# One place each for keys, values and weights of attention in a fused decode block

## The chip, the cores and the metric

One core of a Trainium2 chip runs the kernel. The metric is device time in microseconds of one execution, as the median of several runs; lower is better. The engines named below are TensorE (PE, with its weight loads PEld), VectorE (DVE), ScalarE (ACT), GpSimd (POOL) and the engine that issues most DMAs, SyncE (SP).

## The reference

Four tokens (batch 4, one query each) pass a layer norm. The result feeds two branches, and the output is their sum with the input:

```
xn  = layernorm(x)                                  # [4, 512]
q   = xn @ wq                                       # 32 heads of 128
k,v = the last 4096 positions of the caches         # 8 key/value heads, each serves 4 query heads
o   = softmax(q k^T / sqrt(128)) v
out = x + o @ wo + (silu(xn @ w_gate) * (xn @ w_up)) @ w_down    # F = 1792
```

All inputs are bf16. The kernel reads 8 groups (key/value heads) of 4 MB of K and 4 MB of V, 4 MB each of wq and wo, and 1792 KB each of w_gate, w_up and w_down: 81 MB.

## The kernel before, in words

A group is one key/value head for all four batches. Its K lies in SBUF as 128 partitions by 128 tiles of 128 elements; its V likewise. For each group there is one pass:

- **Keys.** In 16 chunks of 8 tiles TensorE transposes K into PSUM (`transposes`, L436), DVE or ACT copies the chunk to SBUF (L346, L286; every third one is ACT's), and TensorE forms the scores (`scores`, L445) into four PSUM banks, two chunks behind the transposes. DVE takes the maximum of each bank (L350).
- **Values of the group before.** TensorE sums the probabilities (`den`, L453) and multiplies them with V (`pv`, L459, 64 matmuls), with the transpose of the new maxima (L489) after the first 24. Then it adds the negated maxima to the scores as a product with a mask (L493), ACT exponentiates the banks into P (L289), and `sums` (L466, L468) with DVE normalizes the output of the group before.

So K of pass r and V of group r-1 are used in pass r. The first pass runs its values step on a P of ones, with whatever lies in the V place; that result is overwritten. After the loop one more values step does group 7.

K, V and P have two places each, taken in turn by even and odd groups. The first place of V is `vbuf0`; the second is the place of wq, whose name the trace keeps (`wq_sb`). WO is loaded into the first place of K.

SP issues all loads in one order: WQ, X, WG, WU, K 0, K 1, V 0, then K r and V r-1 for r = 2 to 7, then V 7 in two halves, WD, and WO in five parts. A load of K waits until the transposes of the group two before are done (L238, on `s_tr`), a load of V until the product of the group two before is done (L246 and L251, on `s_pv`). SP issues in order: while it waits, nothing behind it is issued. Issued transfers run one behind another.

Ahead of the loop: the layer norm on DVE, the query product (L410) and its transposes, then the gate product and the up product (L423), the gating on ACT and DVE (L281 to L335, on all 512 columns) and the transposes to `guT` (L429). TensorE starts the first keys when `guT` is ready.

Behind the loop: the output is transposed and spread to `OP` (L508, L512, L388), the products with WD (L518) and with the first 16 rows of WO (L526) collect in one bank, which is folded (L531), and the last 16 rows of WO are added (L538). SP stores the result (L272).

Of the kernel before, what the change touches and what calls it, by code (L numbers as in the profile page):

```python
# [5 lines left out]
ALU = mybir.AluOpType  # L6
# [4 lines left out]
def bass_parallel_sum__sliding_block_cached__swiglu_ffn__decode_kernel(  # L11
# [28 lines left out]
    HALF = NT // 2  # L40
    SCALE = float(Dh) ** -0.5
# [7 lines left out]
    WQ = sb("wq_sb", [128, NC, HQ * Dh], BF16)  # L49
    KB = [sb("kbuf%d" % s, [128, NT, Dh], BF16) for s in range(2)]  # L50
    VB0 = sb("vbuf0", [128, NT, Dh], BF16)
# [18 lines left out]
    P = [sb("p%d" % s, [128, NT, CQ], BF16) for s in range(2)]  # L70
    ex = P[0][:, 0:NT // 2, :].rearrange("p t c -> p (t c)").bitcast(FP32)
    gs = P[0][:, NT // 2:, :].rearrange("p t c -> p (t c)").bitcast(FP32)
    gu = KT[1][:, 0:4, :].rearrange("p k d -> p (k d)")
# [76 lines left out]
    s_gu = sem("s_gu")  # L150
# [4 lines left out]
    s_tr = [[sem("s_tr%d_%d" % (g, n)) for n in range(NCH)] for g in range(2)]
    s_ev = [[sem("s_ev%d_%d" % (g, n)) for n in range(NCH)] for g in range(2)]
    s_sc = [[sem("s_sc%d_%d" % (g, q)) for q in range(NB)] for g in range(2)]
    s_sh = [[sem("s_sh%d_%d" % (g, q)) for q in range(NB)] for g in range(2)]
    s_xp = [[sem("s_xp%d_%d" % (g, q)) for q in range(NB)] for g in range(2)]
    s_cm = [sem("s_cm%d" % g) for g in range(2)]  # L160
    s_mt = [sem("s_mt%d" % g) for g in range(2)]
    s_dd = [sem("s_dd%d" % g) for g in range(2)]
    s_pv = [sem("s_pv%d" % g) for g in range(2)]
    s_oc = [sem("s_oc%d" % g) for g in range(2)]
    s_sl = [sem("s_sl%d" % g) for g in range(2)]
    s_nm = [sem("s_nm%d" % g) for g in range(2)]
# [23 lines left out]

    def run_gpsimd(eng):
        for t in (ident, identf, I4, I48, Lsel, sel2, mxd, Dsh, I4w):
            eng.memset(t[:], 0.0)
# [8 lines left out]
                          fill=1.0, base=0, channel_multiplier=1)  # L202
        eng.memset(OP[:], 0.0)
        eng.memset(P[1][:], 1.0)
        eng.drain()
        eng.affine_select(I48[0:16, :], I48[0:16, :], pattern=[[-1, CQ]], compare_op=ALU.not_equal,
                          fill=1.0, base=0, channel_multiplier=1)
        eng.drain()
        eng.affine_select(I48[32:48, :], I48[32:48, :], pattern=[[-1, CQ]], compare_op=ALU.not_equal,
# [24 lines left out]
    def run_sync(eng):  # L234
        def load_k(r):
            if r >= 2:
                eng.wait_ge(s_tr[r % 2][NCH - 1], r // 2)
            eng.dma_start(KB[r % 2][:].rearrange("p t d -> p (t d)"), kv_ap(A_k_cache, r)).then_inc(d_k[r % 2], 16)  # L238

        def load_v(r, half=None):  # L240
            dst = VB[r % 2].rearrange("p t d -> p (t d)")
            src = kv_ap(A_v_cache, r)
            if r == 1:
                eng.wait_ge(s_q, 1)
            if r >= 1 and half != 1:
                eng.wait_ge(s_pv[(r - 1) % 2], (r - 1) // 2 + 1)  # L246
            if half is None:
                eng.dma_start(dst, src).then_inc(d_v[r % 2], 16)
            else:
                n = HALF * Dh  # L250
                eng.dma_start(dst[:, half * n:(half + 1) * n], src[:, :, half * n:(half + 1) * n]).then_inc(  # L251
                    d_vb if half else d_v[r % 2], 16)
# [3 lines left out]
        eng.dma_start(WG[:], wg_ap).then_inc(d_wg, 16)
        eng.dma_start(WU[:], wu_ap).then_inc(d_wu, 16)
        load_k(0)
        load_k(1)
        load_v(0)  # L260
        for r in range(2, HKV):
            load_k(r)
            load_v(r - 1)
        load_v(HKV - 1, 0)
        load_v(HKV - 1, 1)
        eng.dma_start(WD[:], wd_ap).then_inc(d_wd, 16)
        for q, (a, b) in enumerate(ROWS):
            if q == 0:
                eng.wait_ge(s_tr[0][NCH - 1], HKV // 2)
            eng.dma_start(WO[:, a:b, :], wo_ap[:, a:b, :]).then_inc(d_wo[q], 16)  # L270
        eng.wait_ge(s_y, 1)
        eng.dma_start(out_ap, y_ap).then_inc(d_out, 16)  # L272
        eng.wait_ge(d_out, 16)

    def run_scalar(eng):
        eng.wait_ge(s_var, 1)
        eng.activation(st_std[:], st_var[:], ACT.Sqrt).then_inc(s_std, 1)
        eng.wait_ge(s_q, 1)
        eng.copy(qs[:, 1, :], ps_S[1][:]).then_inc(s_qs, 1)
        eng.wait_ge(s_g, 1)  # L280
        eng.activation(ex, gate_ps[:], ACT.Exp, scale=-1.0).then_inc(s_ex, 1)  # L281
        with eng.Fori(0, HKV // 2) as i:
            for g in range(2):
                for n in range(2, NCH, 3):
                    eng.wait_ge(s_tr[g][n], i + 1)
                    eng.copy(KT[n % 3][:], kt_ps[n % 3]).then_inc(s_ev[g][n], 1)  # L286
                for q in range(NB):
                    eng.wait_ge(s_sh[g][q], i + 1)
                    eng.activation(P[g][:, q * TB:(q + 1) * TB, :], S_ps[q], ACT.Exp,  # L289
                                   scale=SCALE).then_inc(s_xp[g][q], 1)  # L290
        eng.wait_ge(s_pt, 1)
        eng.copy(part[64:128, :], part_ps[64:128, :]).then_inc(s_ptc, 1)

    def run_vector(eng):
# [44 lines left out]
        eng.tensor_copy(guT[:, 12:NF, :], gT[:, 3, 16 - NF:, :])
        eng.drain().then_inc(s_guT, 1)  # L340
        for s in s_xp[1] + [s_nm[1]]:
            eng.sem_inc(s, 1)

        def evac(i, g, n):
            eng.wait_ge(s_tr[g][n], i + 1)
            eng.tensor_copy(KT[n % 3][:], kt_ps[n % 3]).then_inc(s_ev[g][n], 1)  # L346

        def bank_max(i, g, q):
            eng.wait_ge(s_sc[g][q], i + 1)
            eng.tensor_reduce(mxb[:, q, :], S_ps[q].rearrange("p t c -> p c t"), AX.X, ALU.max)  # L350

        def sums(sems, v):
            s_v, s_o, s_l, s_n, slot = sems
            eng.wait_ge(s_v, v)
            eng.tensor_copy(o4[:], o4_ps)  # L355
            eng.tensor_tensor(dd[:], fold16[:], den_ps.to_broadcast([128, CQ]), ALU.mult)
            eng.drain().then_inc(s_o, 1)
# [3 lines left out]
            eng.tensor_tensor(slot, ot_ps, rden[:], ALU.mult).then_inc(s_n, 1)

        with nc.Fori(0, HKV // 2, engines=bass.OrderedEngineSet([eng.engine]), hint_back_edge=True) as i:
            for g in range(2):
                for n in range(NCH):
                    if n % 3 != 2:
                        evac(i, g, n)
                    if n in (4, 9, 13):
                        bank_max(i, g, n // 4 - 1)
                bank_max(i, g, NB - 1)  # L370
                eng.drain()
                eng.tensor_reduce(mx1[:], mxb[:].rearrange("p q c -> p c q"), AX.X, ALU.max)
                eng.drain()
                eng.tensor_tensor(mxd[:, 0:64].rearrange("p (e c) -> p e c", c=32)[:, :, 0:CQ], bc(mx1[:], 2), bc(mask[:], 2), ALU.add)
                eng.drain().then_inc(s_cm[g], 1)
# [18 lines left out]
    def run_tensor(eng):  # L394
# [180 lines left out]
```

## Time and profile before

| | us |
|---|---|
| median of 3 runs | 198.8 |
| the runs | 197.3 to 198.88 |
| the profiled execution | 198.41 |
| its span, first to last instruction | 195.5 |
| TensorE matmuls busy | 153.4 |
| DVE busy | 109.7 |
| ACT busy | 61.5 |

The profile is of one execution. Its rows give start, length, engine, line, operation, output and input, and in square brackets how long the engine had been idle and what ended the wait. A matmul's end is modelled. `PEclk` is the granted share of the TensorE clock. The name `kbuf` stands for both places of K, and for WO; `wq_sb` for WQ and for V of odd groups.

### The profile page before, as it was taken

Reading aid. Unit: us, or ns where it says so; the run is one execution under the profiler, and the core shown is the slowest. Engines: PE = TensorE matmul, PEld = TensorE weight load, DVE = VectorE, ACT = ScalarE, POOL = GpSimd, SP = SyncE. Lnnn points to the kernel's source line nnn. Section 1 sums busy time; section 2 is a strip of 40 time slices with the busy share of each in tenths; the row PEclk is TensorE's granted clock in tenths of the full one; section 3 lists DMA queues with packets and bytes.
Section 4 is the critical chain, followed back from the end, with each engine's and each line's share of the span. In section 5 each row is a group of like instructions: output and inputs, shape, how many; then the busy total and the mean of one; then the engine's idle time right before and its main releaser. Section 6 shows DMA issues by size and latency. Waiting matters only on the chain.

```text
span 195.5 us, 6723 instructions
## 1 busy us (share of the span) xinstructions
PE 153.4 (78%) x3063; PEld 125.7 (64%) x3063; DVE 109.7 (56%) x223; ACT 61.5 (31%) x78; POOL 10.1 (5%) x31
## 2 busy tenths in 40 slices
PE   0003894899988798999998999999599959996435
PEld 0002310898788668978976987996599659965213
DVE  0025218478577637866875785886278636851210
ACT  2000310244344235426525443551345133512010
POOL 8740000000000000000000000000000000000000
PEclk9999999589999969999999999999889997999855
DMA  6999999999999999999999999999999999999991
GB/s 221 436 422 427 447 456 429 439 429 432 422 426 426 419 426 429 436 436 429 436 436 429 429 429 429 436 429 429 436 436 429 429 429 429 402 429 422 419 398 72
DMA packets 3780, 81.14 MB, mean 415 GB/s; under 512 B 440, under 2 KB 572, under 8 KB 828
## 3 DMA queue, kind: packets, MB, share of 16 engines
q1 hardware_dynamic: 3772, 81.01, 97.1%
q8 instruction: 7, 0.11, 0.2%
q14 instruction: 1, 0.01, 0.0%
HBM read 81.01 MB, written 0.00 MB: 414 GB/s over the span
## 4 chain that ended last, share of the span: by engine, by line
PE 48%; DMA 34%; DVE 9%; issue 3%; ACT 3%; SPq 1%; DVEq 1%
PE ps_kt L436 22%; DMA kbuf<-in_A_wo_dram 16%; DMA kbuf<-in_A_k_cache_dram 12%; PE ps_s L445 10%; DMA x_sb<-in_A_x_dram 6%; PE ps_o L459 4%; ACT kT L286 3%; PE ps_s L493 2%; PE ps_s L423 2%; PE ps_s L410 2%; DVE p L330 2%; DVE mxb L350 1%; PE ps_s L538 1%; PE ps_s L526 1%; PE ps_o L468 1%
## 5 line engine op out<-in xcount | busy, mean ns | idle before, releaser
L436 PE MATMUL ps_kt<-ident,kbuf 128*128 128x128 bf16 x1024 | 80.4, 228 | 5.0 <-DMA kbuf<-in_A_k_cache_dram 4.1
L346 DVE COPY kT<-ps_kt 128x1024 bf16<-128x1024 bf16 x88 | 59.0, 687 | 20.9 <-PE ps_kt L436 18.6
L436 PEld LDWEIGHTS ps_kt<-ident,kbuf 128*128 128x128 bf16 x1024 | 63.0, 102 | 5.3 <-DMA kbuf<-in_A_k_cache_dram 4.3
L286 ACT COPY kT<-ps_kt 128x1024 bf16<-128x1024 bf16 x40 | 40.5, 1012 | 57.2 <-PE ps_kt L436 57.2
L445 PE MATMUL ps_s<-qT,kT 128*128 x1024 | 45.2, 170 | 5.0 <-ACT kT L286 2.2
L445 PEld LDWEIGHTS ps_s<-qT,kT 128*128 128x128 bf16 x1024 | 38.4, 97 | 8.8 <-issue 3.8
L289 ACT ACTIVATE p<-ps_s 128x512 bf16<-128x512 f32 x32 | 16.5, 603 | 34.7 <-PE ps_s L493 34.7
L350 DVE TENSOR_REDUCE mxb<-ps_s 128x16 f32<-128x512 f32 x32 | 21.9, 686 | 5.4 <-PE ps_s L445 4.6
L400 PE MATMUL ps_s<-i,xn 4*128 4x4 f32 x4 | 0.6, 254 | 17.5 <-DVE xn L311 17.5
L400 PEld LDWEIGHTS ps_s<-i,xn 4*128 4x128 f32 x4 | 0.6, 207 | 17.5 <-issue 17.5
L459 PE MATMUL ps_o<-wq_sb,p 128*32 128x256 bf16 x320 | 10.4, 274 | 0.0
L459 PE MATMUL ps_o<-vbuf,p 128*32 128x256 bf16 x256 | 9.5, 296 | 0.0
L493 PE MATMUL ps_s<-dsh,lsel 128*128 128x512 bf16 x32 | 8.6, 392 | 0.0
L459 PEld LDWEIGHTS ps_o<-wq_sb,p 128*32 128x32 bf16 x320 | 7.7, 96 | 0.7
L459 PEld LDWEIGHTS ps_o<-vbuf,p 128*32 128x32 bf16 x256 | 6.5, 103 | 2.1 <-issue 1.1
L355 DVE COPY o<-ps_o 128x256 f32<-128x256 f32 x9 | 3.8, 425 | 6.7 <-PE ps_o L459 6.7
L297 DVE TENSOR_REDUCE st_sum<-x_sb 4x1 f32<-4x512 bf16 x1 | 0.7, 674 | 12.2 <-DMA x_sb<-in_A_x_dram 12.2
L359 DVE RECIPROCAL rden<-ps_o 128x16 f32<-128x16 f32 x9 | 2.3, 257 | 8.9 <-PE ps_o L468 8.9
L453 PE MATMUL ps_o<-ones,p 128*128 128x1 bf16 x144 | 5.0, 163 | 1.2 <-ACT p L289 1.2
L453 PEld LDWEIGHTS ps_o<-ones,p 128*128 128x128 bf16 x144 | 4.4, 96 | 1.8 <-issue 1.3
L468 PE MATMUL ps_o<-fold,o 128*128 128x16 f32 x36 | 5.4, 263 | 0.0
L493 PEld LDWEIGHTS ps_s<-dsh,lsel 128*128 128x128 bf16 x32 | 2.6, 101 | 4.0 <-DVE dsh L381 1.5
(96 smaller groups left out, 81.4 us busy)
## 6 DMA issues: line engine op xcount, KB each, us to landing
kbuf<-in_A_k_cache_dram SPq DMA_DIRECT2D x8, 4096.0 KB, 22.1
vbuf<-in_A_v_cache_dram SPq DMA_DIRECT2D x4, 4096.0 KB, 29.5
wq_sb<-in_A_v_cache_dram SPq DMA_DIRECT2D x3, 4096.0 KB, 22.7
wq_sb<-in_A_wq_dram SPq DMA_DIRECT2D x1, 4096.0 KB, 12.2
wq_sb<-in_A_v_cache_dram SPq DMA_DIRECT2D x2, 2048.0 KB, 20.4
kbuf<-in_A_wo_dram SPq DMA_DIRECT2D x1, 2048.0 KB, 30.5
wg_sb<-in_B_w_gate_dram SPq DMA_DIRECT2D x1, 1792.0 KB, 16.3
wu_sb<-in_B_w_up_dram SPq DMA_DIRECT2D x1, 1792.0 KB, 20.3
```

What stands on the lines that cost most here:

```text
L286: eng.copy(KT[n % 3][:], kt_ps[n % 3]).then_inc(s_ev[g][n], 1)
L289: eng.activation(P[g][:, q * TB:(q + 1) * TB, :], S_ps[q], ACT.Exp, scale=SCALE).then_inc(s_xp[g][q], 1)
L330: eng.reciprocal(ex, ex)
L346: eng.tensor_copy(KT[n % 3][:], kt_ps[n % 3]).then_inc(s_ev[g][n], 1)
L350: eng.tensor_reduce(mxb[:, q, :], S_ps[q].rearrange("p t c -> p c t"), AX.X, ALU.max)
L410: last = mm(ps_S[j][32 * k:32 * k + 32, :], XnT[:, c, :], WQ[:, c, 512 * (4 * j + k):512 * (4 * j + k) + 512], start=(c == 0), stop=(c == ...
L436: last = eng.transpose(kt_ps[n % 3][:, k, :], KB[g][:, 8 * n + k, :], ident[:])
L445: last = mm(S_ps[q][:, 8 * (n % 4) + k, :], KT[n % 3][:, k, :], QT[:, bass.ds(2 * i + g, 1), :, :].rearrange("p o b h -> p (o b h)"), star ...
L453: mm(den_ps, P[e][:, 8 * u:8 * u + 8, :].rearrange("p t c -> p (t c)"), ones[:, 0:1], start=(u == 0), stop=(u == NT // 8 - 1))
L459: last = mm(o4_ps[32 * k:32 * k + 32, :], P[e][:, 2 * u:2 * u + 2, :].rearrange("p t c -> p (t c)"), VB[e][:, 2 * u:2 * u + 2, :].rearrang ...
L468: last = mm(ot_ps, o4[:, 128 * e:128 * e + 128], fold[:, 16 * e:16 * e + 16], start=(e == 0), stop=(e == 1), skip_group_check=True)
L493: mm(S_ps[q], Lsel[:], bc(Dsh[:], TB), start=False, stop=True, skip_group_check=True).then_inc(s_sh[g][q], 1)
```

## The change

- **One place** each for K, V and P; the loop has one group per pass and eight passes. WQ uses the place of V. WO has its own place, and its load waits for nothing.
- **Loads.** X is issued by ACT. WQ and each K come in two halves; the first half of K r waits for the eighth chunk of pass r-1 to be transposed, the second half for the last. V r waits until pass r has multiplied V r-1 (`s_pv` at r+1). The order is WQ, WG, K 0, WU, then K r and V r-1 for r = 1 to 7, then V 7 whole, WD in four transfers (96, 20 and 10 rows, and 2 rows cut in eight pieces each), WO in five.
- **Tail.** The up product, its transposes and the gating run after pass 7 (block `t_up`); the gate product stays in front, but its activation is taken later, after the transpose, on 64 columns. The values step is one block (`t_values`) for all nine uses; the ninth also runs the maxima's transpose and the mask product on stale data, released by two extra increments of DVE. TensorE's loop is written with blocks and branches. The end is a block (`t_tail`) that runs once, with a branch back to itself that is never taken and carries a branch hint.
- **Set-up.** Memsets of OP, P and others move from POOL to DVE.

```diff
-    KB = [sb("kbuf%d" % s, [128, NT, Dh], BF16) for s in range(2)]
-    VB0 = sb("vbuf0", [128, NT, Dh], BF16)
+    KB = sb("kbuf", [128, NT, Dh], BF16)
+    VB = sb("vbuf", [128, NT, Dh], BF16)
+    WO = sb("wo_sb", [128, 32, D], BF16)
...
-    WO = KB[0][:].rearrange("p t d -> p (t d)").rearrange("p (j n) -> p j n", n=D)
+    WQ = VB[:].rearrange("p t d -> p (t d)").rearrange("p (c n) -> p c n", c=NC)
...
-    P = [sb("p%d" % s, [128, NT, CQ], BF16) for s in range(2)]
+    P = sb("p", [128, NT, CQ], BF16)
...
+        def load_ka(r):
+            if r:
+                eng.wait_ge(s_tr[NCH // 2 - 1], r)
+            eng.dma_start(kf[:, 0:n], kv_ap(A_k_cache, r)[:, :, 0:n]).then_inc(d_ka, 16)
+
+        def load_kb(r):
+            if r:
+                eng.wait_ge(s_tr[NCH - 1], r)
+            eng.dma_start(kf[:, n:], kv_ap(A_k_cache, r)[:, :, n:]).then_inc(d_kb, 16)
+
+        def load_v(r):
+            eng.wait_ge(s_pv, r + 1)
+            eng.dma_start(vf, kv_ap(A_v_cache, r)).then_inc(d_v, 16)
+
+        eng.dma_start(WQ[:, 0:2, :], wq_ap[:, 0:2, :]).then_inc(d_qa, 16)
+        eng.dma_start(WQ[:, 2:4, :], wq_ap[:, 2:4, :]).then_inc(d_v, 16)
         eng.dma_start(WG[:], wg_ap).then_inc(d_wg, 16)
+        load_ka(0)
+        load_kb(0)
         eng.dma_start(WU[:], wu_ap).then_inc(d_wu, 16)
...
+        for r in range(1, HKV):
+            load_ka(r)
+            load_kb(r)
             load_v(r - 1)
...
+        load_v(HKV - 1)
+        for u, v in WDROWS:
+            eng.dma_start(WD[u:v], wd_ap[u:v]).then_inc(d_wd, 16)
+        eng.dma_start(WD[126:128].rearrange("p t n -> p (t n)").rearrange("p (s e) -> p s e", s=8),
+                      wd_ap[126:128].rearrange("p t n -> p (t n)").rearrange("p (s e) -> p s e", s=8)).then_inc(d_wd, 16)
...
     def run_scalar(eng):
+        eng.dma_start(X[:], x_ap).then_inc(d_x, 16)
...
-        eng.activation(ex, gate_ps[:], ACT.Exp, scale=-1.0).then_inc(s_ex, 1)
+        eng.copy(gs[:], gate_ps[:]).then_inc(s_gs, 1)
...
+        eng.wait_ge(s_gt, 1)
+        eng.activation(ex[:], every8(gT_ps), ACT.Exp, scale=-1.0).then_inc(s_ex, 1)
+        eng.wait_ge(s_u, 1)
+        eng.copy(us[:], up_ps[:]).then_inc(s_us, 1)
...
+        eng.sem_inc(s_cm, 1)
+        eng.sem_inc(s_dd, 1)
+        sums(LAST + 1, OT[:, LAST, :])
...
+        with nc.body("t_values", valid_engines=me):
+            i = nc.snap(it, min_val=0, max_val=LAST)
+            eng.wait_ge(d_v, 16 * i + 16)
+            for q in range(NB):
+                eng.wait_ge(s_xp[q], i + 1)
+            eng.wait_ge(s_nm, i + 1)
+            for u in range(NT // 8):
+                mm(den_ps, P[:, 8 * u:8 * u + 8, :].rearrange("p t c -> p (t c)"), ones[:, 0:1],
+                   start=(u == 0), stop=(u == NT // 8 - 1))
+            pv(0, 24)
+            eng.wait_ge(s_cm, i + 1)
+            eng.transpose(mx_ps, mxd[:], identf[:]).then_inc(s_mt, 1)
+            pv(24, 64).then_inc(s_pv, 1)
...
+            nc.regs_alu(it, it, 1, op=ALU.add)
+            eng.br_lt(it, HKV, on_true="t_keys", on_false="t_more")
+        with nc.body("t_more", valid_engines=me):
+            eng.br_lt(it, LAST + 1, on_true="t_up", on_false="t_tail")
...
+            nc.regs_alu(once, once, 1, op=ALU.add)
+            eng.br_lt(once, 1, on_true="t_tail", on_false="t_end").branch_hint(loc)
```

More of the change, by code (lines that the diff above doesn't have):

```diff
@@ L149, in bass_parallel_sum__sliding_block_cached__swiglu_ffn__decode_kernel @@
     s_g = sem("s_g")
[L150 removed]
+    s_gs = sem("s_gs")
     s_gt = sem("s_gt")
     s_u = sem("s_u")
+    s_us = sem("s_us")
+    s_ut = sem("s_ut")
     s_ex = sem("s_ex")
     s_guT = sem("s_guT")
[L155 to L166, printed above, removed]
+    s_tr = [sem("s_tr%d" % n) for n in range(NCH)]
+    s_ev = [sem("s_ev%d" % n) for n in range(NCH)]
+    s_sc = [sem("s_sc%d" % q) for q in range(NB)]
+    s_sh = [sem("s_sh%d" % q) for q in range(NB)]
+    s_xp = [sem("s_xp%d" % q) for q in range(NB)]
+    s_cm = sem("s_cm")
+    s_mt = sem("s_mt")
+    s_dd = sem("s_dd")
+    s_pv = sem("s_pv")
+    s_oc = sem("s_oc")
+    s_sl = sem("s_sl")
+    s_nm = sem("s_nm")
     s_rt = sem("s_rt")
@@ L339, in run_vector, with evac @@
[L339 to L349, printed above, removed]
+        for t in s_xp + [s_nm]:
+            eng.sem_inc(t, 1)
+        def evac(i, n):
+            eng.wait_ge(s_tr[n], i + 1)
+            eng.tensor_copy(KT[n % 3][:], kt_ps[n % 3]).then_inc(s_ev[n], 1)
@@ L359, in sums @@
             eng.reciprocal(rden[:], dn_ps)
             eng.drain()
[L361 to L375, printed above, removed]
-                eng.wait_ge(s_mt[g], i + 1)
-                eng.tensor_reduce(nrm[:], mx_ps[0:48, :], AX.X, ALU.max, negate=True)
-                eng.drain()
-                eng.tensor_scalar(Dsh[0:48, :], I48[:], nrm[:, 0:1], None, ALU.mult)
-                eng.drain()
-                eng.scalar_tensor_tensor(Dsh[32:48, :], I48[32:48, :], nrm[32:48, 0:1], Dsh[32:48, :],
-                                         ALU.mult, ALU.subtract).then_inc(s_dd[g], 1)
-                sums((s_pv[g], s_oc[g], s_sl[g], s_nm[g], OT[:, bass.ds(2 * i + g, 1), :].rearrange("p o c -> p (o c)")), i + 1)
@@ L427, in run_tensor @@
-        eng.wait_ge(s_gu, 1)
-        for t in range(4):
-            last = eng.transpose(gT_ps[:, t, :], gu[:, 128 * t:128 * t + 128], ident[:])
-        last.then_inc(s_gt, 1)
-        def transposes(i, g, n):
+                    m = mm(o[32 * k:32 * k + 32, :].rearrange("p (t m) -> p t m", m=128), XnT[:, c, :],
+                           w[:].rearrange("p c (m t) -> p c t m", t=NF)[:, c, T0[k]:T0[k] + 4, :],
+                           start=(c == 0), stop=(c == NC - 1), skip_group_check=True)
@@ L433, in transposes @@
+            return m
+        eng.wait_ge(d_wg, 16)
+        x_times(WG, gate_ps).then_inc(s_g, 1)
+        def transposes(i, n):
             if n == 0:
-                eng.wait_ge(d_k[g], 16 * i + 16)
+                eng.wait_ge(d_ka, 16 * i + 16)
+            if n == NCH // 2:
+                eng.wait_ge(d_kb, 16 * i + 16)
             for k in range(8):
-                last = eng.transpose(kt_ps[n % 3][:, k, :], KB[g][:, 8 * n + k, :], ident[:])
-            last.then_inc(s_tr[g][n], 1)
@@ L462, in pv @@
             return last
-        def sums(s_o, s_l, v):
-            eng.wait_ge(s_o, v)
+        me = bass.OrderedEngineSet([eng.engine])
+        it = nc.alloc_registers("t_i", engines=me)
+        once = nc.alloc_registers("t_once", engines=me)
+        nc.regs_mov(it, 0)
+        nc.regs_mov(once, 0)
+        eng.wait_ge(s_qc, 1)
+        eng.wait_ge(s_gs, 1)
+        nc.br("t_keys", engines=me)
+        with nc.body("t_up", valid_engines=me):
+            for t in range(4):
+                last = eng.transpose(gT_ps[:, 128 * t:128 * t + 128], gs[:, 128 * t:128 * t + 128], identf[:])
+            last.then_inc(s_gt, 1)
+            eng.wait_ge(d_wu, 16)
+            x_times(WU, up_ps).then_inc(s_u, 1)
+            eng.wait_ge(s_us, 1)
+            for t in range(4):
+                last = eng.transpose(uT_ps[:, 128 * t:128 * t + 128], us[:, 128 * t:128 * t + 128], identf[:])
+            last.then_inc(s_ut, 1)
+            nc.br("t_values", engines=me)
@@ new lines, in run_tensor @@
+        with nc.body("t_keys", valid_engines=me):
+            i = nc.snap(it, min_val=0, max_val=HKV - 1)
+            transposes(i, 0)
+            transposes(i, 1)
+            for n in range(NCH):
+                if n + 2 < NCH:
+                    transposes(i, n + 2)
+                scores(i, n)
+            nc.br("t_values", engines=me)
+        with nc.body("t_values", valid_engines=me):
+            i = nc.snap(it, min_val=0, max_val=LAST)
+            eng.wait_ge(d_v, 16 * i + 16)
+            for q in range(NB):
+                eng.wait_ge(s_xp[q], i + 1)
+            eng.wait_ge(s_nm, i + 1)
[6 more added lines that the diff above has]
+            pv(24, 64).then_inc(s_pv, 1)
+            eng.wait_ge(s_dd, i + 1)
+            for q in range(NB):
+                mm(S_ps[q], Lsel[:], bc(Dsh[:], TB), start=False, stop=True,
+                   skip_group_check=True).then_inc(s_sh[q], 1)
+            eng.wait_ge(s_oc, i + 1)
@@ L496, in run_tensor @@
-        last = HKV // 2
-        for q in range(NB):
-            eng.wait_ge(s_xp[1][q], last + 1)
-        eng.wait_ge(d_v[1], 16 * (last + 1))
-        eng.wait_ge(s_nm[1], last + 1)
-        den(1)
-        pv(1, 0, 32)
-        eng.wait_ge(d_vb, 16)
-        pv(1, 32, 64).then_inc(s_pv[0], 1)
-        mm(part_ps[0:32, :], I4w[:], X[:], start=True, stop=False, skip_group_check=True)
-        sums(s_oc[0], s_sl[0], last + 1)
-        eng.wait_ge(s_nm[0], last + 1)
-        eng.transpose(rt_ps, OT[:, 1:, :].rearrange("p r c -> p (r c)"), ident[:]).then_inc(s_rt, 1)
```

279 lines of the change are left out of this document (129 added, 150 removed).

## The prediction

> **What bounds the kernel now.** I read the page first: busy shares, DMA slices, queues.
>
> ```profile
> span 195.5 us, 6723 instructions
> ...
> DMA  6999999999999999999999999999999999999991
> ...
> q1 hardware_dynamic: 3772, 81.01, 97.1%
> ...
> PE 48%; DMA 34%; DVE 9%; issue 3%; ACT 3%; SPq 1%; DVEq 1%
> ```
>
> The kernel's one data queue keeps the 16 DMA engines busy for 97.1% of the span, short only in the first and the last slice. 81 MB must be moved before and after, so a gain can come only from the missing 2.9% (5.7 us), and any hole in the queue is paid in full. The table of stages puts a rate to it, one group of heads to a row, after a row from the start:
>
> ```profile
> 24.44:39.10 14.66, 11.32 (x87) 5.07 (x80) 7.20 (x9) 1.61 (x2) 0.00 (x0) 0.83 1.03 441
> 97.75:117.30 19.55, 18.28 (x421) 16.34 (x419) 14.54 (x28) 8.41 (x11) 0.00 (x0) 1.00 1.00 431
> 139.80:159.25 19.45, 16.96 (x347) 15.29 (x347) 12.07 (x24) 7.12 (x9) 0.00 (x0) 0.91 1.00 431
> 159.25:178.70 19.45, 17.84 (x387) 16.08 (x391) 12.02 (x24) 7.12 (x9) 0.00 (x0) 0.91 1.00 426
> ```
>
> The last two columns are DMA share and GB/s: no idle. TensorE is second, and the timeline shows its room:
>
> ```profile
> 89.26 1.50 PE L436 MATMUL ps_kt<-ident,kbuf 128*128 128x128 bf16 x24
> 104.79 0.60 PE L468 MATMUL ps_o<-fold,o 128*128 128x16 f32 x4
> 105.24 1.50 PE L436 MATMUL ps_kt<-ident,kbuf 128*128 128x128 bf16 x24
> 139.83 2.71 PE L436 MATMUL ps_kt<-ident,kbuf 128*128 128x128 bf16 x24 [2.04 <-DMA kbuf<-in_A_k_cache_dram]
> ```
>
> A pass that waits for nothing goes from 89.26 to 105.24: 16.0 us. Before 139.83 TensorE waits for K 6, and before 159.27 (quoted below) for K 7: landings 19.44 us apart, so 9.72 us for each 4 MB. The chain of waits names TensorE for 48%, because TensorE works off a backlog from its late start until about 139. That is not the bound: the queue was full all the while. I turned next to what the queue's own engine waits for:
>
> ```profile
> SPq L238 <- PE ps_kt L436: 102.0, 6, 43.1
> SPq L251 <- PE ps_o L459: 18.8, 1, 18.8
> ```
>
> These cost nothing now, as the next rows show: K loads need a median 22.1 us from issue to landing, against 12.2 us for the first load, issued to an empty queue. The difference is queueing behind other transfers. That cover is what the change spends.
>
> ```profile
> kbuf<-in_A_k_cache_dram SPq DMA_DIRECT2D x8, 4096.0 KB, 22.1
> wq_sb<-in_A_wq_dram SPq DMA_DIRECT2D x1, 4096.0 KB, 12.2
> wg_sb<-in_B_w_gate_dram SPq DMA_DIRECT2D x1, 1792.0 KB, 16.3
> wu_sb<-in_B_w_up_dram SPq DMA_DIRECT2D x1, 1792.0 KB, 20.3
> ```
>
> **One place for V: the hole near the end.** In the new order V 7 follows V 6 directly, and both go to the same place. V 7 may be issued only when pass 7 has multiplied V 6 (s_pv at 8). WD and WO stand behind that wait on SP, so nothing fills the queue. Before, V 7 had the other place. The price is built from these rows, one pass's values step and the transfer it releases:
>
> ```profile
> 152.63 0.54 PE L453 MATMUL ps_o<-ones,p 128*128 128x1 bf16 x16
> 154.33 1.27 PE L459 MATMUL ps_o<-wq_sb,p 128*32 128x256 bf16 x40
> 155.65 1.18 SPq L251 DMA_DIRECT2D wq_sb<-in_A_v_cache_dram  x2
> 159.27 1.76 PE L436 MATMUL ps_kt<-ident,kbuf 128*128 128x128 bf16 x24 [2.08 <-DMA kbuf<-in_A_k_cache_dram]
> 68.78 2.32 PE L459 MATMUL ps_o<-vbuf,p 128*32 128x256 bf16 x40
> ```
>
> - Denominator and PV: 152.63 to 155.60, 2.97 us at the full clock. The x40 block also appears at 2.32 instead of 1.27 us; the whole step at that pace is about 5.0 us. TensorE will have waited a while for V 6, and after the 2.08 us wait 24 transposes took 1.76 us, not 1.50. I take 3.8, nearer to the fast row.
> - Issue follows the end of PV by 0.05 us (155.60 to 155.65).
> - A transfer into an empty queue lands 12.2 us after issue against 9.72 in stream: 2.5 us of latency, hidden until now.
>
> V 6 lands at 159.27 + 9.72 = 169.0 in both orders, since the bytes ahead of it are the same. The hole is 3.8 + 0.05 + 2.5 = **6.3 us** (5.5 to 7.5).
>
> The other loads into single places are covered. V of a middle group becomes free 3 to 5 us after its landing, plus 2.5 of latency: 5.5 to 7.5, under the 9.72 that the next K needs on the queue. K's first half is free halfway through a keys step and wanted a V transfer later. So passes 2 to 6 stay at the 19.45 us pace. Zero, with 2 us of cover or more.
>
> **The start.** X moves to ACT's queue, the query product starts on half of WQ, gating and the up product leave the front, and POOL's memsets move to DVE. Queries and memsets are covered: keys wait for WG's product anyway, and WQ lands 12.2 us after its issue, ahead of WG; uncovered, the memsets would cost their own length. The queue order becomes WQ, WG, K 0, WU, K 1. Pass 0 starts earlier, but it must now release K 1's place in time:
>
> ```profile
> 1.67 0.35 SPq L256 DMA_DIRECT2D wg_sb<-in_B_w_gate_dram  x1
> 2.06 0.59 SPq L257 DMA_DIRECT2D wu_sb<-in_B_w_up_dram  x1
> 23.86 3.82 PE L423 MATMUL ps_s<-wg_sb,xnT 128*32 128x512 bf16 x16
> 22.07 0.58 ACT L279 CAST kT<-ps_s 128x512 bf16<-128x512 f32 x1 [5.47 <-PE ps_s L410]
> 35.06 2.74 PE L436 MATMUL ps_kt<-ident,kbuf 128*128 128x128 bf16 x24 [0.86 <-DVEq L340]
> 41.69 0.61 PE L436 MATMUL ps_kt<-ident,kbuf 128*128 128x128 bf16 x8
> 47.08 0.61 PE L436 MATMUL ps_kt<-ident,kbuf 128*128 128x128 bf16 x8
> 50.58 1.27 PE L459 MATMUL ps_o<-wq_sb,p 128*32 128x256 bf16 x40
> ```
>
> WG lands at 1.67 + 16.3 = 17.97. Its product takes 3.82, and keys now also wait for ACT's copy of it (s_gs), 0.58 by the nearest row: 22.4. K 0's first half lands 4.86 after WG, at 22.8, so keys start near 22.9 instead of 35.06. Offsets of pass 0 before: eighth chunk transposed after 7.24 us (42.30), last chunk after 12.63 (47.69), PV done after 16.79 (51.85).
> - K 1a: issue at 30.1, landing 2.5 + 4.86 later at 37.5. An unbroken queue would land WU at 32.1 (22.36 before, plus 9.72) and K 1a at 36.9. Hole 0.6.
> - K 1b: issue at 35.5, landing 42.9 against 42.4. Hole 0.5.
> - V 0: issue at 39.7, landing 51.95 against 52.6. No hole.
>
> Together **1.1 us**. Pass 0 began slowly: seven chunks from 35.06 to 41.69, 0.95 us each, then eight to 47.08, 0.67 each. If the gate product leaves the clock high, 2 us go and the holes vanish; if V 1 is late too, they reach 2.
>
> **The tail.** The up product, transposes and gating now run between pass 7 and V 7's landing: a 3.8 us product and small steps within a transfer of 12.2 us. [...] The ninth values step adds a mask product ahead of its sums:
>
> ```profile
> 155.53 1.04 PE L493 MATMUL ps_s<-dsh,lsel 128*128 128x512 bf16 x4
> 156.42 0.33 PE L466 MATMUL ps_o<-dd,onesf 128*128 128x16 f32 x2
> 178.12 1.93 PE L459 MATMUL ps_o<-wq_sb,p 128*32 128x256 bf16 x64
> 180.69 0.39 PE L466 MATMUL ps_o<-dd,onesf 128*128 128x16 f32 x2 [0.32 <-DVEq L357]
> 183.17 1.04 PE L518 MATMUL ps_s<-wd_sb,guT 128*32 128x512 bf16 x14
> 188.10 1.90 PE L526 MATMUL ps_s<-kbuf,oP 128*32 128x512 bf16 x16 [3.88 <-DMA kbuf<-in_A_wo_dram]
> 193.09 0.11 PEld L538 LDWEIGHTS ps_s<-kbuf,oP 128*32 128x32 bf16 x4 [0.20 <-DMA kbuf<-in_A_wo_dram]
> ```
>
> Sums start 0.82 after PV with the mask product (155.60 to 156.42), 0.64 without (180.05 to 180.69): 0.2. From V 7's landing TensorE needs 3 to 5 for PV, 0.25 for the stale transpose, then 4.16 (180.05 to 184.21) + 0.2: ready for WO after 7.6 to 9.6. WO's first part came 9.4 after V 7 (188.10 against 178.7). Zero; 0.5 at the most. The end after the last WO part, 193.09 to 195.5, is unchanged.
>
> **W_down in four parts** (96, 20, 10 and 2 rows, the last cut in eight). The engines do not finish together now:
>
> ```profile
> 191.00:192.00 1.00, 1.00 (x40) 0.96 (x32) 0.00 (x0) 0.00 (x0) 0.00 (x0) 0.50 0.49 187
> 192.00:193.10 1.10, 1.10 (x44) 0.63 (x35) 0.00 (x0) 0.00 (x0) 0.00 (x0) 0.50 0.16 56
> ```
>
> Idle share 0.51 x 1.0 + 0.84 x 1.1 = 1.4 us per engine: the most that a better split could gain. Against it, one WD row is 14 KB and takes an engine 0.53 us at 431/16 GB/s; two extra rows on some engine cost 1.07. The hole before V 7 lets every engine run dry and start level, so an unevenness gathered earlier is gone when WD comes. I take 0 (-1.4 to +1.07).
>
> K and WQ in halves: the stage with V 7 in halves took the same 19.45 us as the one before. Zero.
>
> **Sum.** 6.3 + 1.1 = 7.4 us on the profiled execution. That took 198.41 us with a span of 195.5, so 2.9 lie around the span; it stands 0.4 below the median 198.8. 198.41 + 7.4 = **205.8**, span 202.9.
>
> **Rivals.**
> - *The overlap pays for the hole (not slower).* TensorE starts 12 us earlier and is never behind, and the chain gives it 48%. If TensorE were the pace, those 12 us would cover the 7.4: bounded by the queue's missing 5.7 us, of which the first latency 2.5 and the end 2.4 stay, it gives 197.6 to 198.4. It decides if the DMA share in the middle stages falls below 0.97 now; they show 1.00. 0.05.
> - *Passes become TensorE-paced (slower still).* Eight loop edges instead of four, jumps between blocks, and two waits per pass that may lower the clock. A pass from a cold start (139.83, 159.27) takes about 17.3 of 19.45; a further 2.1 us per pass uses up the room. With 3 us, 7 passes lose 0.9 each: 212. Against it: at the loop edge between 104.79 + 0.60 and 105.24 TensorE loses nothing. 0.07. [...]
> - *The queue runs faster* with level engines: 81 MB at the 441 GB/s of the quoted early stretch take 4.3 us less than at 431, so 201.5. Later stages don't hold it. 0.03.
> - *Two engines carry two WD rows more.* From a level start they end the last transfer 1.07 us later: 206.9. It lies inside the forecast; for it: 20 and 10 rows do not divide by 16; against: how rows fall on engines is in no row here. 0.25 of the forecast's 0.80. [...]
>
> **Numbers.** Forecast 0.80 with its own range: 198.41 + 5.5 - 1.4 = 202.5 at the low end, 198.41 + 7.5 + 2.0 + 0.5 + 1.07 = 209.5 at the high. Outcomes not named, 0.05. The range 202.5 to 209.5 leaves out about 2 in 10. The runs before spread by 0.8%, so 1% is about what can be told from no change: faster 0.03, same 0.05, slower 0.92.
>
> **What would show it.** One slice of DMA share near 0 around 170 to 176, with SP's longest late wait at V's load ending on PV; V 7 landing 15 to 17.5 us after V 6; smaller dips at 30 to 38; middle stages at 1.00; up and gating finished before V 7 lands. No hole there would overturn the prediction; a middle share under 0.95 would mean passes are TensorE-paced.

## The result

| | before | after |
|---|---|---|
| median, us | 198.05 | 214.53 |
| runs, us | 196.97 to 198.88 | 214.16 to 216.69 |
| profiled execution, us | 198.41 | 216.69 |
| its span, us | 195.5 | 215.4 |

The ratio is 1.085 (95% interval 1.077 to 1.094): slower, as forecast, but by 16.5 us instead of 7.4, and outside the range of 202.5 to 209.5. The profiled execution is the slowest of the after runs, 2.2 us above their median.

The page of the changed kernel:

```profile
span 215.4 us, 6817 instructions
...
DMA  6999998999999999999999999999999806999892
GB/s 241 435 436 437 414 408 341 365 432 411 420 441 444 399 429 450 420 417 426 399 411 438 411 432 408 420 389 432 402 426 450 365 6 274 408 292 199 243 400 84
...
q1 hardware_dynamic: 4938, 81.01, 92.9%
...
DMA 71%; PE 22%; issue 3%; SPq 2%; ACT 0%; DVE 0%
```

One slice of DMA share is 0: the hole that was forecast. Three slices further on the rate falls to 292, 199 and 243 GB/s while the share still reads 9, 9 and 8 tenths. That was not forecast. SyncE's waits (total, times, longest) name PV as what V's loads wait for, and the timeline of TensorE and SyncE dates both:

```profile
SPq L253 <- PE ps_o L471: 62.6, 8, 18.6
```

```profile
174.47 0.54 PE L514 MATMUL ps_o<-ones,p 128*128 128x1 bf16 x16 [1.78 <-DMA vbuf<-in_A_v_cache_dram]
176.06 2.33 PE L471 MATMUL ps_o<-vbuf,p 128*32 128x256 bf16 x40
178.43 0.54 SPq L253 DMA_DIRECT2D vbuf<-in_A_v_cache_dram  x1
191.28 0.66 PE L514 MATMUL ps_o<-ones,p 128*128 128x1 bf16 x16 [5.31 <-DMA vbuf<-in_A_v_cache_dram]
203.35 1.89 PE L549 MATMUL ps_s<-wd_sb,guT 128*32 128x512 bf16 x14 [3.92 <-DMA wd_sb<-in_B_w_down_dram]
207.98 1.90 PE L557 MATMUL ps_s<-wo_sb,oP 128*32 128x512 bf16 x16 [2.74 <-DMA wo_sb<-in_A_wo_dram]
```

TensorE's waits mark landings: V 6 at 174.47, V 7 at 191.28, WD at 203.35, the first part of WO at 207.98. WD takes 12.1 us behind V 7; at the 431 GB/s of the kernel before, its 1792 KB take 4.3. The span grew by 19.9 us, which splits as follows:

- V 6 lands 5.5 late against 169.0.
- The hole costs 16.8 - 9.72 = 7.1.
- WD costs 12.1 - 4.3 = 7.8.
- Up to WO's first part 0.5 is gained (9.4 - 4.3 = 5.1 before, 4.63 now). From there to the end both take 7.4.

The stages show what kind of loss each is (last three columns: clock, DMA share, GB/s):

```profile
33.00:38.00 5.00, 3.73 (x103) 3.38 (x100) 3.36 (x7) 1.01 (x1) 0.00 (x0) 1.00 0.83 338
38.00:43.00 5.00, 4.66 (x87) 3.44 (x75) 2.39 (x9) 2.37 (x5) 0.00 (x0) 1.00 0.99 354
117.30:139.80 22.50, 20.19 (x388) 16.18 (x387) 12.71 (x27) 7.12 (x9) 0.00 (x0) 0.80 1.00 419
174.00:179.00 5.00, 4.53 (x83) 2.85 (x84) 1.30 (x6) 0.04 (x1) 0.00 (x0) 0.68 0.00 0
190.94:195.20 4.26, 3.92 (x73) 2.69 (x77) 0.00 (x0) 0.00 (x0) 0.00 (x0) 0.50 1.08 252
195.20:203.20 8.00, 3.62 (x44) 2.06 (x36) 1.87 (x6) 0.00 (x0) 0.00 (x0) 0.71 0.96 162
```

In the hole the engines stand still (share 0.00). Under WD their share is full (1.08, 0.96) while they move 252 and 162 GB/s: busy, but slow. Engines that had merely run out of rows would show as a low share, as in the kernel before at 192.00 (0.16). Against 431 GB/s, the two rows of the start (33 to 43) fall short by (93 + 77) x 5 us = 0.85 MB, or 2.0 us.

### The profile page after: what moved, and what is told of

Its sections match the earlier page's. It is cut to its first block, busy times and chain, and to the rows that moved or that the text cites. A ratio compares the mean times of both kernels' runs of the same rounds, so it can differ in the third digit from the quotient of the medians.

```text
span 215.4 us, 6817 instructions
## 1 busy us (share of the span) xinstructions
PE 165.7 (77%) x3072; PEld 127.2 (59%) x3072; DVE 108.9 (51%) x229; ACT 62.4 (29%) x81; POOL 7.7 (4%) x25
## 4 chain that ended last, share of the span: by engine, by line
DMA 71%; PE 22%; issue 3%; SPq 2%; ACT 0%; DVE 0%
DMA vbuf<-in_A_v_cache_dram 49%; DMA wo_sb<-in_A_wo_dram 12%; PE ps_o L471 12%; DMA kbuf<-in_A_k_cache_dram 9%; PE ps_kt L453 3%; PE ps_o L514 2%; PE ps_s L462 2%; PE ps_kt L518 1%; PE ps_s L569 1%; PE ps_s L557 1%; SPq L267 1%; ACT kT L288 0%; DVE part L404 0%; PE ps_s L562 0%; SPq L253 0%
## 5 line engine op out<-in xcount | busy, mean ns | idle before, releaser
L453 PE MATMUL ps_kt<-ident,kbuf 128*128 128x128 bf16 x1024 | 75.3, 218 | 2.9 <-issue 1.7
L453 PEld LDWEIGHTS ps_kt<-ident,kbuf 128*128 128x128 bf16 x1024 | 58.7, 97 | 4.9 <-DMA kbuf<-in_A_k_cache_dram 3.0
L462 PE MATMUL ps_s<-qT,kT 128*128 x1024 | 44.5, 170 | 6.4 <-DVE kT L346 4.1
L462 PEld LDWEIGHTS ps_s<-qT,kT 128*128 128x128 bf16 x1024 | 37.4, 96 | 10.6 <-issue 5.5
L291 ACT ACTIVATE p<-ps_s 128x512 bf16<-128x512 f32 x32 | 16.5, 603 | 55.4 <-PE ps_s L522 55.4
L471 PE MATMUL ps_o<-vbuf,p 128*32 128x256 bf16 x576 | 30.5, 383 | 0.0
L471 PEld LDWEIGHTS ps_o<-vbuf,p 128*32 128x32 bf16 x576 | 18.3, 129 | 6.5 <-issue 1.6
L514 PE MATMUL ps_o<-ones,p 128*128 128x1 bf16 x144 | 5.2, 164 | 17.8 <-DMA vbuf<-in_A_v_cache_dram 16.8
L522 PE MATMUL ps_s<-dsh,lsel 128*128 128x512 bf16 x36 | 13.0, 499 | 0.0
L375 DVE TENSOR_REDUCE nrm<-ps_kt 48x1 f32<-48x128 f32 x8 | 2.3, 284 | 18.7 <-PE ps_kt L518 18.7
L358 DVE RECIPROCAL rden<-ps_o 128x16 f32<-128x16 f32 x9 | 2.3, 258 | 12.1 <-PE ps_o L527 12.1
L522 PEld LDWEIGHTS ps_s<-dsh,lsel 128*128 128x128 bf16 x36 | 3.4, 116 | 7.1 <-issue 6.0
L525 PEld LDWEIGHTS ps_o<-dd,onesf 128*128 128x128 f32 x18 | 3.8, 221 | 2.4 <-issue 1.1
```

Of the source, the lines that this page charges most:

```text
L291: eng.activation(P[:, q * TB:(q + 1) * TB, :], S_ps[q], ACT.Exp, scale=SCALE).then_inc(s_xp[q], 1)
L453: last = eng.transpose(kt_ps[n % 3][:, k, :], KB[:, 8 * n + k, :], ident[:])
L462: last = mm(S_ps[q][:, 8 * (n % 4) + k, :], KT[n % 3][:, k, :], QT[:, bass.ds(i, 1), :, :].rearrange("p o b h -> p (o b h)"), start=(n % 4 ...
L471: last = mm(o4_ps[32 * k:32 * k + 32, :], P[:, 2 * u:2 * u + 2, :].rearrange("p t c -> p (t c)"), VB[:, 2 * u:2 * u + 2, :].rearrange("p t ...
L514: mm(den_ps, P[:, 8 * u:8 * u + 8, :].rearrange("p t c -> p (t c)"), ones[:, 0:1], start=(u == 0), stop=(u == NT // 8 - 1))
L522: mm(S_ps[q], Lsel[:], bc(Dsh[:], TB), start=False, stop=True, skip_group_check=True).then_inc(s_sh[q], 1)
```

## The experiments

My theory after the result: the hole is as forecast, WD's transfers are slow in themselves, and a hole of 2 to 3 us at the start is the rest. Rivals stand in each expectation. Each ratio is against runs of the kernel before on the same chip. The medians come from four runs each, twelve for the last kernel, and only two for the 64 and 64 rows and the halves of columns.

| kernel | median us | ratio to before (95%) |
|---|---|---|
| the changed kernel | 214.53 | 1.085 (1.077 to 1.094) |
| WD in one transfer | 208.4 | 1.058 (1.049 to 1.067) |
| WD in 96 and 32 rows | 211.07 | 1.069 (1.061 to 1.077) |
| WD in 64 and 64 rows | 212.19 | 1.073 (1.065 to 1.081) |
| WD in two halves of columns | 207.32 | 1.048 (1.040 to 1.056) |
| kernel before, WD in four | 204.95 | 1.038 (1.029 to 1.046) |
| kernel before, V 7 waits | 206.84 | 1.050 (1.044 to 1.056) |
| own place for V 7 | 200.57 | 1.017 (1.009 to 1.025) |
| V in halves | 203.55 | 1.027 (1.023 to 1.032) |
| WD ahead of V 7 | 205.23 | 1.042 (1.035 to 1.049) |
| a transfer more at the start | 208.8 | 1.056 (1.051 to 1.061) |
| V in halves, WD at the start | 200.83 | 1.013 (1.007 to 1.020) |
| own place, WD at the start | 199.67 | 1.0095 (1.006 to 1.013) |

All but the two kernels named "before" are the changed kernel with the edit, and all of these but the 96 and 32, the 64 and 64 and the halves of columns have WD in one transfer.

**WD in one transfer.**

```diff
-        for u, v in WDROWS:
-            eng.dma_start(WD[u:v], wd_ap[u:v]).then_inc(d_wd, 16)
...
+        eng.dma_start(WD[:], wd_ap).then_inc(d_wd, 16)
```

> The changed kernel with WD in one transfer of 128 rows. Theory A: WD's four transfers are themselves slow; between V 7 and the end of WD the queue is busy but moves only 200 to 300 GB/s, and WD takes about 12.3 us from V 7's landing where the kernel before needs 4.3. Then this run takes 8 us less than the changed kernel, 206.5. Rival B (the term of the prediction): the split only loads two engines with two rows more, 1.07 us; then it takes 213.5, and the slow stretch stays.

Measured 208.4: 6.1 less by the medians, 5.4 by the ratios, where 8 were expected, and 10.0 less in the spans of the profiled executions (205.4 against 215.4). Of these 10.0, 7.7 lie behind V 7, whose way to WO is 9.0 us now (16.7 in the changed kernel); 2.5 lie ahead of V 6, which lands at 171.99 instead of 174.47; the hole is 0.2 longer. The stage between V 7 and WD runs at full rate:

```profile
189.03 0.62 PE L511 MATMUL ps_o<-ones,p 128*128 128x1 bf16 x16 [5.58 <-DMA vbuf<-in_A_v_cache_dram]
198.04 1.05 PE L554 MATMUL ps_s<-wo_sb,oP 128*32 128x512 bf16 x16 [0.23 <-DMA wo_sb<-in_A_wo_dram]
```

```profile
188.70:193.00 4.30, 3.97 (x73) 2.77 (x77) 0.00 (x0) 0.00 (x0) 0.00 (x0) 0.50 1.00 430
```

Theory A holds, B falls. Why the medians show less than the 7.7 of the traces is open; the four runs of this kernel spread over 3 us.

**Rows or pieces?** The same place in the code, with these transfers:

```diff
+        eng.dma_start(WD[0:96], wd_ap[0:96]).then_inc(d_wd, 16)
+        eng.dma_start(WD[96:128], wd_ap[96:128]).then_inc(d_wd, 16)
```

> WD in two transfers of 96 and 32 rows, with every row whole and both counts multiples of 16. Theory A1: a transfer of fewer than 128 partitions is slow because its engines write into the same part of SBUF; then WD takes 7 to 8.5 us and the time is 3 to 4 us above that of WD in one transfer, about 210. Theory A2: it was slow because 20, 10 and 2 rows reach only some engines, or because the last two rows are cut into small pieces; then this run equals WD in one transfer, 206.5. [...]

```diff
+        eng.dma_start(WD[0:64], wd_ap[0:64]).then_inc(d_wd, 16)
+        eng.dma_start(WD[64:128], wd_ap[64:128]).then_inc(d_wd, 16)
```

> WD in two transfers of rows 0 to 63 and 64 to 127. If adjoining partitions share a way into SBUF (theory A1), each half is slow although all 16 engines carry four whole rows: WD takes 7 to 8.5 us from V 7's landing, like the 96 and 32 rows (8.3). If a transfer is slow only where rows per engine are no multiple of what 128 rows give, 64 rows are the tamer case: 5 us or less.

```diff
+        for h in range(2):
+            eng.dma_start(WD[:, 7 * h:7 * h + 7, :], wd_ap[:, 7 * h:7 * h + 7, :]).then_inc(d_wd, 16)
```

> WD in two transfers that each have all 128 rows and half of the columns. Theory A1: no loss, 4.3 us from V 7's landing to WD's, as in one transfer. Rival: splitting itself costs, 1 us or more.

Halves of columns lose nothing (207.32); both splits by rows do (212.19 and 211.07, against 208.4 in one transfer). TensorE in the kernel with 64 and 64 rows, and its first product with WO in the kernel with halves of columns:

```profile
190.07 0.75 PE L512 MATMUL ps_o<-ones,p 128*128 128x1 bf16 x16 [5.67 <-DMA vbuf<-in_A_v_cache_dram]
198.54 1.89 PE L547 MATMUL ps_s<-wd_sb,guT 128*32 128x512 bf16 x14 [0.38 <-DMA wd_sb<-in_B_w_down_dram]
203.42 1.90 PE L555 MATMUL ps_s<-wo_sb,oP 128*32 128x512 bf16 x16 [2.98 <-DMA wo_sb<-in_A_wo_dram]
```

```profile
189.76 0.57 PE L512 MATMUL ps_o<-ones,p 128*128 128x1 bf16 x16 [4.78 <-DMA vbuf<-in_A_v_cache_dram]
199.18 1.05 PE L555 MATMUL ps_s<-wo_sb,oP 128*32 128x512 bf16 x16
```

With 64 and 64 rows WD takes 8.5 us, twice 4.3, and WO comes 13.4 us after V 7. With halves of columns WO is there without a wait 9.4 us after V 7. For the 96 and 32 rows, the table of stages 188 to 190 and 190 to 196:

```profile
188.00:190.00 2.00, 0.53 (x16) 0.52 (x16) 0.00 (x0) 0.00 (x0) 0.00 (x0) 0.50 1.24 287
190.00:196.00 6.00, 6.00 (x82) 3.59 (x78) 0.50 (x2) 0.00 (x0) 0.00 (x0) 0.59 1.01 226
```

Again full share at half the rate (1.01 at 226 GB/s, where WD in one transfer showed 1.00 at 430), with whole rows in counts that divide by 16. So A2 is not what makes them slow, though it may add to the loss of the four transfers. The split into halves of columns cost nothing. What was slow in these runs are WD's transfers into fewer than 128 partitions, and where their stage was read the share was full.

A1 adds a reason, that the engines meet at the same way into SBUF. That was my guess, and it is not shown: no run reads the same rows of WD into other partitions, so a cause on the side of HBM is not excluded. The 96 rows were about as slow for their size as 64: at 226 GB/s their 1.38 MB take an estimated 6.1 us, and each 64 rows took about 4.3, half of the 8.5. That the four transfers take 12.1 us and these two 8.5 is not taken apart further; the 20, 10 and 2 rows were not tried singly.

**The same transfers in the kernel before.** The edit is the four transfers of the change in place of one.

> The kernel before with nothing changed but WD in the four transfers. Theory A: the loss belongs to the transfers, not to the new order around them, so the kernel before loses 7 to 8 us: about 206. Rival B: the uneven rows use the spread between the engines' ends that the kernel before shows: 197 to 199.

Measured 204.95 against 196.97, 8.0 us more. Where V 7 and WD are loaded the engines are busy at about half the rate:

```profile
182.00:186.00 4.00, 3.87 (x39) 2.55 (x39) 0.50 (x2) 0.00 (x0) 0.00 (x0) 0.50 1.07 237
```

Theory A holds: the loss needs neither the hole nor the new loop, and what spread the engines have does not pay for it.

**Own place for V 7.**

```diff
+    VL = sb("vlast", [128, NT, Dh], BF16)
...
-        load_v(HKV - 1)
+        eng.dma_start(VL[:].rearrange("p t d -> p (t d)"), kv_ap(A_v_cache, HKV - 1)).then_inc(d_vl, 16)
```

> WD in one transfer, and a place of its own for V 7, whose load then waits for nothing but the queue; the ninth values step is a copy that reads it, without the stale transpose and mask product. Theory: the hole before V 7 (about 7 us) goes: 199.5 to 200.5, with no slice of DMA share near 0. Rival: the work of TensorE behind V 7 sets the end, and the hole was partly hidden: 203 or more.

Measured 200.57. In the stretch that held the hole the queue is full:

```profile
172.00:178.00 6.00, 5.46 (x99) 3.43 (x95) 2.51 (x9) 0.28 (x1) 0.00 (x0) 0.72 1.01 437
```

That is 7.8 us less than WD in one transfer, so the hole was paid in full; the stale transpose and mask product, which this kernel also leaves out, are 0.45 by the forecast's terms.

**The wait alone, in the kernel before.**

```diff
+            if r == HKV - 1 and half == 0:
+                eng.wait_ge(s_pv[1], HKV // 2)
```

> The kernel before, with one wait added: V 7's first half is issued only after V 6 has been multiplied, as in the changed kernel. Theory: the hole alone costs 6.5 to 7.5 us here too: 203.5 to 204.5. Rival: the hole is a matter of the changed loop (its clock, its branches): under 4 us, 201 or less.

Measured 206.84, 9.2 more: a hole, and a larger one than expected. The stage and TensorE's wait for V 7:

```profile
169.40:174.50 5.10, 4.71 (x125) 3.69 (x122) 3.56 (x10) 1.01 (x1) 0.00 (x0) 1.00 0.00 0
```

```profile
182.16 0.57 PE L455 MATMUL ps_o<-ones,p 128*128 128x1 bf16 x16 [6.38 <-DMA wq_sb<-in_A_v_cache_dram]
```

Here K is not split, and the keys of the last pass began late, with K 7's landing at 159.71: TensorE is busy through the hole, with keys still to do when V 6 lands. The values step with V 6 starts at 171.23, and V 7 is issued at 174.24. My expectation left that out.

**V in halves.**

```diff
+            eng.wait_ge(s_pa, r + 1)
+            eng.dma_start(vf[:, 0:n], kv_ap(A_v_cache, r)[:, :, 0:n]).then_inc(d_v, 16)
             eng.wait_ge(s_pv, r + 1)
+            eng.dma_start(vf[:, n:], kv_ap(A_v_cache, r)[:, :, n:]).then_inc(d_w, 16)
...
+            pv(24, 32).then_inc(s_pa, 1)
+            eng.wait_ge(d_w, 16 * i + 16)
+            pv(32, 64).then_inc(s_pv, 1)
```

> WD in one transfer, V in two halves as K has: the values step raises a first semaphore after 32 of its 64 matmuls, which releases the place of the first half, and needs the second half of V only then. Theory: the hole before V 7 is the latency of landing, PV and issue in a row; with the first half released before the second has landed, about 1 of 7 us stays: 202 to 203. Rival: the hole stays, since TensorE's work behind V 7 or the whole of PV sets it: 207 to 208.

Measured 203.55, 0.5 above the range. Most of the hole goes. What stays:

```profile
163.00:174.00 11.00, 10.62 (x258) 9.62 (x260) 8.72 (x16) 4.05 (x4) 0.00 (x0) 0.99 0.80 338
174.00:177.00 3.00, 3.00 (x54) 2.10 (x50) 1.31 (x6) 1.69 (x4) 0.00 (x0) 1.00 0.55 175
```

Idle 0.20 x 11 + 0.45 x 3 = 3.5 us, not 1: TensorE is busy throughout, so the first half of V 6 waits for keys before it is multiplied and released.

**WD ahead of V 7.**

```diff
-        load_v(HKV - 1)
         eng.dma_start(WD[:], wd_ap).then_inc(d_wd, 16)
+        load_v(HKV - 1)
```

> WD in one transfer, issued ahead of V 7, so that it fills 4.3 of the 7 us of the hole. Theory: V 7 lands when it did, and then TensorE's work behind it (9.4 us to the products with WO, 5.3 from there to the result, as with WD in one transfer behind V 7) sets the end: a gain under 1 us, 207 to 208.4. Rival: the order of transfers alone sets the end: 4.3 us less, 204.

Measured 205.23, by the ratios 1.6% or 3.2 us under WD in one transfer. Both statements miss. V 7 does land when it did (189.12 beside 189.03), but TensorE then needs 12.1 us to its last product. With WD in one transfer it needed 14.3, and my expectation had 14.7 to the result. WO no longer keeps it waiting:

```profile
189.12 0.69 PE L511 MATMUL ps_o<-ones,p 128*128 128x1 bf16 x16 [5.37 <-DMA vbuf<-in_A_v_cache_dram]
198.04 1.05 PE L554 MATMUL ps_s<-wo_sb,oP 128*32 128x512 bf16 x16
200.12 1.08 PE L566 MATMUL ps_s<-wo_sb,oP 128*32 128x128 bf16 x64
```

**The start.**

```diff
         eng.dma_start(WU[:], wu_ap).then_inc(d_wu, 16)
+        eng.dma_start(FILL[:], wu_ap).then_inc(d_fill, 16)
```

> WD in one transfer, and at the start one transfer more: w_up is loaded a second time, into a place that nothing reads, between WU and the first half of K 1. It moves 1792 KB more, 4.3 us. Theory: the queue runs dry by 2.5 to 3 us around K 1 and V 0, because TensorE releases their places late; the added transfer fills that, and the time grows by 1.3 to 1.8: 210. Rival: the 3 us were lost to the spread between engines or to the rate, and the queue had no hole: it grows by 4.3, 212.7.

Measured 208.8, ratio 1.056 beside 1.058 without the added 4.3 us of transfer; by the profiled spans 2.0 more (207.4 and 205.4). Growth by 4.3 us, the rival, would be a ratio of 1.080, outside the interval. The same stages as above, with the filler:

```profile
33.00:38.00 5.00, 4.67 (x92) 4.38 (x90) 3.21 (x6) 1.54 (x2) 0.00 (x0) 0.74 1.01 422
38.00:43.00 5.00, 4.86 (x99) 3.68 (x96) 2.43 (x10) 2.06 (x4) 0.00 (x0) 1.00 1.03 433
```

The hole is there. By the spans the filler fits into 2.3 us of it; the runs do not tell this growth from none.

**All together.** Both kernels load WD where the filler stood. One has V in halves, as above:

```diff
         eng.dma_start(WU[:], wu_ap).then_inc(d_wu, 16)
+        eng.dma_start(WD[:], wd_ap).then_inc(d_wd, 16)
```

> V in halves, and WD in one transfer moved to the start, between WU and K 1, where it fills the hole. Theory: 2 to 2.5 us of the hole at the start are filled, and at the end TensorE's work behind V 7 (about 12 us to the result when WO waits in the queue no longer) takes over from the transfers: 2 us less than V in halves alone, 201 to 202. Rival: no change against V in halves alone, 203.5.

The other has V 7 in its own place, in halves:

```diff
+        eng.dma_start(lf[:, 0:n], kv_ap(A_v_cache, HKV - 1)[:, :, 0:n]).then_inc(d_vl, 16)
+        eng.dma_start(lf[:, n:], kv_ap(A_v_cache, HKV - 1)[:, :, n:]).then_inc(d_vm, 16)
```

> All three losses undone in the new order: a place of its own for V 7, loaded in halves, and WD in one transfer at the start. Theory: no hole near the end, the start's hole filled, no slow transfer, so the queue is as full as in the kernel before: 197 to 199 beside 197 to 198 of the kernel before, no difference to 1%. Rival: something else of the change costs too, then 200 or more.

Measured 200.83, a little better than expected, and 199.67, above the expected 197 to 199 and short of the rival's 200. With its three losses undone the new order is 0.6 to 1.3% behind the kernel before, and does not beat it. What is left is in TensorE's row, not in the queue's:

```profile
181.38 3.83 PE L439 MATMUL ps_kt<-wu_sb,xnT 128*32 128x512 bf16 x16
186.41 0.54 PE L536 MATMUL ps_o<-ones,p 128*128 128x1 bf16 x16
186.88 1.93 PE L471 MATMUL ps_o<-vlast,p 128*32 128x256 bf16 x64
```

PV of V 7 starts without a wait for the load: the up product and its transposes, free while the hole hid them, now stand ahead of it. That this is the whole of the last 1.6 us (199.67 to 198.02) is argued, not shown. V 6 also lands at 174.19 there, 0.9 later than 169.0 and WD's 4.3 us ahead of it would give.

## Why the prediction missed

- **W_down in four parts** is the step that failed: "I take 0 (-1.4 to +1.07)". It cost 7.8 us in the profile, 6.1 by the medians, 8.0 in the kernel before. I had counted rows per engine and given each row the 0.53 us of a full transfer. In these runs that price held for WD in one transfer into 128 partitions (430 GB/s), not for the four: at share 1.08 the queue moved 252 GB/s. The rival "two engines carry two rows more" shares the mistake. No run shows its 1.07 us, which also stands in the high end of the range, nor how rows fall on engines; what the runs showed in its place is a rate of 252 and 162 GB/s at full share. With WD in one transfer the kernel takes 208.4, inside the range but 2.6 above the 205.8 forecast; the start and the hole are what is left.
- **The hole**: 6.3 forecast (5.5 to 7.5), 7.1 measured, and 7.8 when it is removed. Its terms: PV 3.8 against 3.9 (174.47 to 178.39), issue 0.05 against 0.04, V 7 used 12.85 after issue against 12.2. The mechanism was right.
- **The start**: 1.1 forecast (0 to 2), and mis-sized. V 0 landed at 55.62, not at 52.6; in the six other profiled kernels with the same start it landed between 54.84 and 55.81. With WD in one transfer V 6 is 3.0 late, nearly all of it from the start. The forecast had K 1a issued at 30.1 and K 1b at 35.5; SyncE issued them at 27.40 and 34.69. K 1a was early: the clock was up, and the first 24 transposes took 1.51 us at a granted clock of 1.00 (22.3 to 24.0), against 2.74 before at 0.50 (35.0 to 37.8). The forecast named that case and had the holes vanish with it. They did not, since TensorE then stalled with nothing to wait for that the profile shows:

```profile
30.18 0.38 PE L453 MATMUL ps_kt<-ident,kbuf 128*128 128x128 bf16 x4 [1.75 <-issue]
36.97 0.51 PE L514 MATMUL ps_o<-ones,p 128*128 128x1 bf16 x15 [0.93 <-issue]
55.62 0.54 PE L514 MATMUL ps_o<-ones,p 128*128 128x1 bf16 x16 [2.37 <-DMA vbuf<-in_A_v_cache_dram]
```

  V 0 was issued as forecast (39.77 against 39.7) and still landed 3.0 late. That the transfers around it lost so much, with a share of 0.99 at 354 GB/s, is not settled.
- **The middle**: zero forecast, and right but for this one execution. From V 0's landing to V 6's it took 118.85 us; the eight other profiled kernels that load V 0 to V 6 whole into one place took 117.14 to 117.21, and six rounds of 19.45 are 116.7. The 1.7 us that stand out lie in two rounds of 20.4 and 20.3 us. The chain of waits shows V's load and PV in turn there:

```profile
119.75 15.25 DMA vbuf<-in_A_v_cache_dram
...
137.70 2.29 PE ps_o L471 x39
139.98 0.02 issue
140.00 14.65 DMA vbuf<-in_A_v_cache_dram
```

  It does not show that the cover was used up. These loads took 2.1 to 2.7 us longer to land than the 12.5 of V 7 into an empty queue, so other transfers still stood ahead of them, and the share in that stage is 1.00, at 419 GB/s. Nor is it the slow PV: with 96 and 32 rows the x40 block took 2.32 us too (at 57.67), and the next V landed 19.5 us after the last. Why this execution moved less at a full share stays open; it is 2.2 us above the median, so the median may not hold this loss.
- **The tail**: zero, and right while the hole lasts. TensorE waited 3.92 us for WD. Once the cover goes, as in the last kernel, the tail stands in TensorE's row.
- **The rivals**: the overlap did not pay for the hole, and the queue was not faster. Nor were passes paced by TensorE: the share in the middle stages stayed at 0.98 to 1.00, above the 0.95 that the forecast named as the sign. That V 7 came 16.8 us after V 6, inside the 15 to 17.5, is the mechanism and not luck. That the kernel with WD in one transfer still lies inside the range is owed to the range's width: the start came out about 2 us above its forecast.

## What to carry to other kernels

Here a single buffer cost next to nothing where other transfers stood in the queue between its release and its next load (V 0, V 1 and V 2 came 19.52 and 19.54 us apart, where the pace before is 19.45), and 7.1 us where none stood there, at the last load of the loop. Look at that load, and give it a place of its own: that took 7.8 us off. If a load into SBUF must be split, try columns first: WD took 207.32 in halves of columns, 212.19 in halves of rows, 208.4 whole. To judge a DMA loss, read share and GB/s together: here the hole showed as share 0.00 at 0 GB/s, the slow transfers as 1.08 at 252 GB/s. And before a loss in one profiled execution is explained, look for it in the other profiles of the same code.

## What the runs showed of the hardware

- WD in two transfers, each into 64 adjoining partitions, took 8.5 us in all, twice the 4.3 that its 1792 KB take at 431 GB/s. In two of 128 partitions with half of the columns it lost nothing (207.32 against 208.4). In one transfer of 128 partitions the engines moved 430 GB/s over the 4.3 us behind V 7.
- A transfer of 4 MB issued to an empty queue landed 12.5 us after issue and was used after 12.85 (V 7), where the landings of K 6 and K 7 in the kernel before, 19.44 us apart with a V between them, give 9.72 for each in stream.
- TensorE's slow pace followed a wait of under 2 us in some places and not in others: after 1.78 us idle at 174.47 the x40 block took 2.33 us, at a granted clock of 0.50 (176.0 to 178.4); after 0.93 us idle at 36.97 it took 1.27, at 1.00 (38.4 to 39.7); with a place of its own for V 7 it took 2.21 after 0.54 us idle at 173.02. In the kernel before it takes 1.27 where nothing was waited for. What decides it is not shown.
